# Key rows and row sums of v from TensorE with 0/1 matrices, in place of a DRAM staging copy

## The chip, the cores and the metric

The kernel runs on one core of a Trainium2 chip. The metric is the device time of one execution in microseconds, taken as the median of several runs. The profile is one further execution with the hardware profiler on.

## The reference

Three stages, each of which feeds the next. Only the first one is touched here.

```python
# q, k, v: (4, 8, 576, 64): batch, heads, sequence, head width
q_d, k_d, v_d = (t.reshape(B, H, 144, 4, 64).mean(axis=3) for t in (q, k, v))
out_d  = softmax(q_d @ k_d.T / 8) @ v_d          # each row repeated 4 times
local  = where(abs(i - j) < 4, q @ k.T / 8, -1e9)
x      = repeat(out_d, 4) + softmax(local) @ v   # -> (2304, 512) tokens
g = x @ w_gate; x = (silu(g) * (x @ w_val)) @ w_out          # 512 -> 1536 -> 512
h = x @ w_in;   out = (max(h,0) + alpha*min(h,0)) @ w2_out   # 512 -> 2048 -> 512
```

So for v the first stage needs two things: the sums of four neighbouring rows (for the coarse attention), and, for each query, the seven key rows around it (for the local attention).

## The kernel before

**Attention.** Work comes in units: unit n is one pair of heads and half a sequence (288 rows). There are 4 units per half sequence and 32 in all. The first sequence is units 0 to 7: units 0 to 3 are the first half of its four head pairs, 4 to 7 the second half. They are called the prologue here and are written out by `a_all`: transposes of k and q on TensorE (`a_T`, L283 and L286, L292 for units 4 to 7), scores (`a_QK`, L334 local and L338 coarse, then L343 to L360), exponentials (`a_EXP`, L368 and L377), row sums and normalisation with the 32x32 transposes into the block diagonal tile bd (`a_NRM`, L386 to L408), the transpose of the coarse weights (`a_PT`, L415, L418), and the products with v (`a_PV`, L435 coarse, L439 local, L443 to L449), whose result goes as a high and a low part (xh, xl) to the next stage.

**The two forms of v.** The local product L439 takes vw: for each block of 24 queries the 32 rows of v around it, four blocks in the 128 partitions. `stage(b)` writes these windows for the whole sequence b into a DRAM tensor, vwin (L246 to L261), and `a_load_w` reads them back, two DMAs a unit (L237). The coarse product L435 takes vs, sums of four rows of v: `a_load_v` loads v again as 72 rows of four (tile vd, L216), and `a_vd` adds them on GpSimd (L321, L322), for units 0 to 3; units 4 to 7 use the same sums.

**The order at the start.** SyncE's queue is in order and carries every DMA: k and q of units 0 to 3 (L202, L207), stage(0), the four vd, the windows (L237) and the weights of the first four of twelve column groups j (L103, L105; three tiles g, v, o of 512 KB for each j). Each weight tile is split on arrival into a high and a low part (`w_split`): ScalarE L126, VectorE L127 and L128, ScalarE L131, GpSimd L132. The main loop takes, for each block of 288 tokens and each j, 12 matmuls for gate (L462 to L464), 12 for value and 12 for the output product, with VectorE L502 and L508 between them. A scheduler with a model of the chip's times fixes the order of instructions on each engine beforehand, within the dependences and a few gates; on the chip each engine keeps that order.

**Buffers.** PSUM holds four tiles of two banks for the prologue, one for each of units 0 to 3; units 4 to 7 share three of them, so that unit 7 comes after unit 4. In SBUF the prologue lives in weight slots that are not loaded yet: `order` is g4 v4 o4 g5 (q and vw), v5 o5 g6 v6 (qs: transposed q, scores, results), o6 g7 v7 o7 (k, later q and vw of units 4 to 7), g8 v8 o8 g9 (vd, later qs of units 4 to 7), v9 o9 g10 v10 (bd). A weight tile is loaded once its slot is given back.

Of the kernel before, what the change touches and what calls it, by code (L numbers as in the profile page):

```python
# [8 lines left out]
F32 = mybir.dt.float32  # L9
# [3 lines left out]
ALU = mybir.AluOpType  # L13
# [4 lines left out]

K = dict(kdP=0, qdP=0, dnP=2, ldn=9, lo='asvw0123', NPRO=8, c=5, a1=1, a2=0, OFF=25, oT=3, oE=3, oP=5, oV=11, vd1=2, vd2=1, pre=(1, 1, 0, 0), lo1=0, lo2=1, nst=3, nrm=0, sub=0, nrm1=0, sub1=0, qtA=0, ldw=1, xl1=0, ly=4, l2=3, st2=2, early=1, w2p=1, la=0, bdV=0, sp=9, s2=0, s3=0, gj=7, gs=1, vr=0, kc=0, gD=(0, 0, 0, 0, 0, 0), gP=(0, 2, 8, 8, 0, 0), gA=(0, 0, 0, 0, 0, 0))


@with_exitstack
def attn_moe_moe2_kernel(
# [113 lines left out]
    pbd = {}  # L137
    kds = {}
    vss = {}
    vds = {}  # L140
    bds = [ap_.tile([128, 2, NW, 128], F32, name=f"bd{i}", bufs=1) for i in range(NBD)]

    def coords(n):
        blk, hp = divmod(n, NP)
        b, half = divmod(blk, 2)
        return b, half, hp, blk
# [1 line left out]
    order = [f"{kind}{j}" for j in range(F1 - 8, F1) for kind in "gvo"]  # L148
    st_slots = order[5 * NP:][:K["nst"]]
    NEARLY = F1 - 2  # L150
    pslot = {(what, n): order[4 * i + n] for i, what in enumerate(("qv", "qs", "kn", "vd", "bd")) for n in range(NP)}
    for n in range(NP):
        pslot["qv", n + NP] = pslot["kn", n]
        pslot["qs", n + NP] = pslot["qs" if K["vr"] else "vd", n]
    NPRO = K["NPRO"]
    srs = [ap_.tile([128, 8], F32, name=f"sr{i}", bufs=1) for i in range(4)]

    def at_(n, shape, tag):
        return wp.tile(shape, F32, tag=pslot[tag, n], name=tag)
# [23 lines left out]
    def a_load(n):  # L183
        b, half, hp, blk = coords(n)
        h0, t0 = 2 * hp, half * HB
        d = hu[n] = {}
        if n >= NPRO:

            loads = [("qn", q, HB, t0)]
            if half == 0:  # L190
                loads.insert(0, ("kn", k, S, 0))
            for tag, src, rn, r0 in loads:
                t = d[tag] = ap_.tile([128, rn], F32, tag=tag, name=tag, bufs=1)
                for i in range(4):
                    nc.sync.dma_start(
                        out=t[32 * i:32 * (i + 1)].rearrange("r (m c) -> r m c", c=32),
                        in_=src[b, h0 + i // 2, r0:r0 + rn, 32 * (i % 2):32 * (i % 2 + 1)].rearrange("(m r) c -> r m c", r=32))
            return
        if half == 0:
            kn = d["kn"] = at_(n, [QB, 6, 2, D], "kn")  # L200
            for h in range(2):
                nc.sync.dma_start(out=kn[:, :, h], in_=k[b, h0 + h].rearrange("(r p) c -> p r c", p=QB))  # L202
        t = at_(n, [128, 2 * NW * 2 * D], "qv").rearrange("p (a w h c) -> p a w h c", a=2, w=NW, h=2)
        d["vw"] = t[:, 1]
        qn = d["qn"] = t[:QB, 0]
        for h in range(2):
            nc.sync.dma_start(out=qn[:, :, h], in_=q[b, h0 + h, t0:t0 + HB, :].rearrange("(r p) c -> p r c", p=QB))  # L207

    def a_load_v(n):
        b, half, hp, blk = coords(n)  # L210
        h0 = 2 * hp
        if half == 0:
            hu[n]["vd"] = []
            if n < NP:
                vd = vds[hp] = at_(n, [72, 2, 2, 4 * D], "vd")
                nc.sync.dma_start(out=vd.rearrange("p h f x -> p (h f) x"),  # L216
                                  in_=v[b, h0:h0 + 2].rearrange("h (f p r) c -> p (h f) (r c)", f=2, r=4))
            for f in range(2):
                if n < NP:
                    hu[n]["vd"].append(vd[:, :, f])  # L220
                    continue
                vf = ap_.tile([72, 2, 4 * D], F32, tag="vd", name="vd", bufs=NVD)
                hu[n]["vd"].append(vf)
                nc.sync.dma_start(out=vf, in_=v[b, h0:h0 + 2, f * HB:(f + 1) * HB].rearrange("h (p r) c -> p h (r c)", r=4))

    def a_load_w(n):

        b, half, hp, blk = coords(n)
        if n < NP:
            pbd[n] = at_(n, [128, 2, NW, 128], "bd")  # L230
            (nc.vector if K["bdV"] else nc.gpsimd).memset(pbd[n], 0.0)
        if n >= NPRO:
            hu[n]["vw"] = ap_.tile([128, NW, 2, D], F32, tag="vw", name="vw", bufs=NVW)
        t = hu[n]["vw"]
        for h in range(2):
            w0 = ((b * H + 2 * hp + h) * 2 + half) * NW * 128
            nc.sync.dma_start(out=t[:, :, h], in_=vwin[w0:w0 + NW * 128, :].rearrange("(w p) c -> p w c", p=128))  # L237

    def stage(b):

        nw = H * S // SUB
        g0, g1, ng = b * nw, (b + 1) * nw, B * nw

        def win(a, e):
            n = (e - a) * SWIN
            nc.sync.dma_start(  # L246
                out=vwin[a * SWIN:e * SWIN, :].rearrange("(g r) c -> g (r c)", r=SWIN),
                in_=bass.AP(v.tensor, v.offset + (a * SUB - 3) * D, [[SUB * D, e - a], [1, SWIN * D]]))

        vf = v.rearrange("b h s c -> (b h s) c")  # L250
        if g0 == 0:
            nc.sync.dma_start(out=vwin[0:3, :], in_=vf[0:3, :])
            nc.sync.dma_start(out=vwin[3:SWIN, :], in_=vf[0:SWIN - 3, :])
            win(1, 16)
            g0 = 16
        if g1 == ng:
            win(g0, g1 - 16)
            win(g1 - 16, g1 - 1)
            r0, m = (g1 - 1) * SWIN, SUB + 3
            nc.sync.dma_start(out=vwin[r0:r0 + m, :], in_=vf[B * H * S - m:, :])  # L260
            nc.sync.dma_start(out=vwin[r0 + m:r0 + SWIN, :], in_=vf[0:SWIN - m, :])  # L261
        else:
            win(g0, g1)
# [48 lines left out]

    def a_vd(n):
        b, half, hp, blk = coords(n)
        if n < NPRO and K["vr"]:
            return
        if half == 0:
            vs = vss[hp] = ap_.tile([72, 2, 2, D], F32, tag=f"vs{hp}", name="vs", bufs=1)
            for f in range(2):
                vv = hu[n]["vd"][f].rearrange("p h (r c) -> p h r c", r=4)  # L320
                nc.gpsimd.tensor_tensor(out=vv[:, :, 0:2], in0=vv[:, :, 0:2], in1=vv[:, :, 2:4], op=ALU.add)  # L321
                nc.gpsimd.tensor_tensor(out=vs[:, f], in0=vv[:, :, 0], in1=vv[:, :, 1], op=ALU.add)  # L322

    def a_QK(n, A):
        b, half, hp, blk = coords(n)
# [94 lines left out]
    def a_PV(n, A):  # L420
        b, half, hp, blk = coords(n)
        d = hu[n]
        pt, vw, bd = d["pt"], d["vw"], d["bd"]
        if n < NPRO and K["vr"]:
            vd = vds[hp].rearrange("p h f (r c) -> p h f r c", r=4)
            for f in range(2):
                for r in range(4):
                    for h in range(2):
                        nc.tensor.matmul(A[64 * h:64 * h + 64, 1, 0:QD], vd[:, h, f, r], pt[:, h, f * QD:(f + 1) * QD],
                                         start=(f == r == 0), stop=(f == 1 and r == 3))  # L430
        else:
            vs = vss[hp]
            for f in range(2):
                for h in range(2):
                    nc.tensor.matmul(A[64 * h:64 * h + 64, 1, 0:QD], vs[:, f, h], pt[:, h, f * QD:(f + 1) * QD],  # L435
                                     start=(f == 0), stop=(f == 1))
        for w in range(NW):
            for h in range(2):
                nc.tensor.matmul(A[64 * h:64 * h + 64, 0, w * QB:(w + 1) * QB], vw[:, w, h],  # L439
# [31 lines left out]
    def load1(j):  # L471
        for kind in "gvo":
            w_load(kind, j, f"{kind}{j}")
# [144 lines left out]

    if True:
        make_identity(nc, ident)  # L620
        for tok in K["lo"]:
            if tok == "s":
                stage(0)
            elif tok in "avw":
                for n in range(NP):
                    {"a": a_load, "v": a_load_v, "w": a_load_w}[tok](n)
            elif tok == "x":
                for n in range(NP):
                    a_load_v(n)
                    a_load_w(n)  # L630
            else:
                load1(int(tok))
        for t in srs:
            nc.vector.memset(t, 1.0)

# [17 lines left out]
        P = [ATT, Y[0], Y[1], pgv.tile([128, 2, 512], F32, name="gv")]  # L653
        def a_all(n, A):
            a_T(n, A)
            if K["vd1"] == 0:
                a_vd(n)
            a_QK(n, A)
            gate(n, 0)
            if K["vd1"] == 1:  # L660
                a_vd(n)
            a_EXP(n)
            a_NRM(n)
            gate(n, 1)
            if K["vd1"] == 2:
                a_vd(n)
            a_PT(n, A)
            if K["vd1"] == 3:
                a_vd(n)
            a_PV(n, A)  # L670

        pc = [0]
# [13 lines left out]
        GV[1] = pg2.tile([128, 512], F32, name="v")  # L686
        for n in range(NP, NPRO):
            a_load(n)
            a_load_w(n)
        for n in range(NP, NPRO):  # L690
            if n == NP + 2:
                preps(K["pre"][2])
# [141 lines left out]
```

## Time and profile before

| | |
|---|---|
| median of 3 runs | 1025.0 us (1024.01 to 1026.19) |
| the profiled execution | 1022.0 us |
| span of its profile | 1020.1 us |
| TensorE busy | 970.3 us, 95% |
| VectorE, GpSimd, ScalarE busy | 496.7, 387.7, 292.3 us |

The shares are means over the whole span. The prologue and the first block of the main loop, roughly the first 150 us, look quite different from the rest, and the rows further down are mostly from there. A matmul's duration in the trace includes its latency, so a TensorE that is "busy" is not one at its peak.

### The profile page before, as it was taken

Reading aid. Unit: us, or ns where it says so; the run is one execution under the profiler, and the core shown is the slowest. Engines: PE = TensorE matmul, PEld = TensorE weight load, DVE = VectorE, ACT = ScalarE, POOL = GpSimd, SP = SyncE. Lnnn points to the kernel's source line nnn. Section 1 sums busy time; section 2 is a strip of 40 time slices with the busy share of each in tenths; the row PEclk is TensorE's granted clock in tenths of the full one; section 3 lists DMA queues with packets and bytes.
Section 4 is the critical chain, followed back from the end, with each engine's and each line's share of the span. In section 5 each row is a group of like instructions: output and inputs, shape, how many; then the busy total and the mean of one; then the engine's idle time right before and its main releaser. Section 6 shows DMA issues by size and latency. Waiting matters only on the chain.

```text
span 1020.1 us, 19253 instructions
## 1 busy us (share of the span) xinstructions
PE 970.3 (95%) x7760; PEld 867.5 (85%) x7760; DVE 496.7 (49%) x1045; ACT 292.3 (29%) x660; POOL 387.7 (38%) x492
## 2 busy tenths in 40 slices
PE   5388789999999999999999999999999999999997
PEld 4288789999999999999999998888888888888896
DVE  5898884546453646353532769722322322322232
ACT  3656542222222222222223656312101101111111
POOL 5868773233422343322223335724223322322222
PEclk9999999999999999999999999999999999999999
DMA  8996751123120232110103884102000100100010
GB/s 199 289 305 217 196 139 39 35 67 60 42 51 16 54 71 45 38 29 15 43 13 88 290 265 127 42 1 62 21 0 19 55 1 1 42 11 0 1 43 21
DMA packets 135895, 77.81 MB, mean 76 GB/s; under 512 B 97407, under 2 KB 127103, under 8 KB 135039
## 3 DMA queue, kind: packets, MB, share of 16 engines
q1 hardware_dynamic: 135804, 76.58, 27.0%
q8 instruction: 60, 0.98, 0.4%
q14 instruction: 31, 0.25, 0.1%
HBM read 67.12 MB, written 15.73 MB: 81 GB/s over the span
## 4 chain that ended last, share of the span: by engine, by line
PE 79%; DVE 7%; DMA 6%; SPq 4%; issue 2%; POOL 2%; ACT 1%; DVEq 0%; POOLq 0%; ACTq 0%
PE y L599 6%; PE y L601 6%; PE y L600 6%; PE g L462 6%; PE v L463 6%; PE v L462 5%; PE g L464 5%; PE g L463 5%; PE v L464 5%; PE y L462 4%; PE y L464 4%; PE y L463 4%; PE h L462 3%; PE h L464 3%; PE h L463 3%
## 5 line engine op out<-in xcount | busy, mean ns | idle before, releaser
L587 POOL TENSOR_TENSOR gl<-t,gh 128x512 fp32r<-128x512 f32 (+1 forms) x80 | 97.0, 1214 | 250.6 <-ACT gh L586 244.1
L462 PE MATMUL g<-xh,w 128*128 128x288 f32 x384 | 117.0, 305 | 13.4 <-DVE u L502 8.8
L586 ACT CAST gh<-t 128x512 fp32r<-128x512 f32 (+1 forms) x80 | 46.1, 578 | 278.4 <-DVE t L583 239.0
L463 PE MATMUL y<-pl,w 128*128 128x288 f32 x384 | 114.3, 300 | 3.2 <-POOL pl L512 3.2
L462 PE MATMUL v<-xh,w 128*128 128x288 f32 x384 | 116.5, 303 | 0.0
L463 PE MATMUL v<-xl,w 128*128 128x288 f32 x384 | 116.0, 302 | 0.0
L464 PE MATMUL g<-xh,w 128*128 128x288 f32 x384 | 114.6, 298 | 1.2 <-POOL w L132 1.2
L464 PE MATMUL v<-xh,w 128*128 128x288 f32 x384 | 114.7, 299 | 0.0
L463 PE MATMUL g<-xl,w 128*128 128x288 f32 x384 | 114.6, 298 | 0.0
L599 PE MATMUL y<-w,gh 128*128 128x512 f32 x288 | 113.2, 393 | 1.0 <-ACT sy L531 1.0
L502 DVE SCALAR_TENSOR_TENSOR u<-u,g 128x288 f32<-128x288 f32 x96 | 43.3, 451 | 144.2 <-ACT u L501 144.1
L464 PE MATMUL y<-ph,w 128*128 128x288 f32 x384 | 113.5, 298 | 0.0
L600 PE MATMUL y<-w,gh 128*128 128x512 f32 x288 | 112.8, 392 | 0.0
L601 PE MATMUL y<-w,gl 128*128 128x512 f32 x288 | 112.0, 392 | 0.0
L462 PE MATMUL y<-ph,w 128*128 128x288 f32 x384 | 111.2, 303 | 0.3 <-ACT ph L511 0.3
L512 POOL TENSOR_TENSOR pl<-u,ph 128x288 fp32r<-128x288 f32 x96 | 80.8, 842 | 56.0 <-ACT ph L511 55.7
L132 POOL TENSOR_TENSOR w<-st,w 128x512 fp32r<-128x512 f32 x52 | 73.8, 1425 | 59.5 <-ACT w L131 57.8
L462 PEld LDWEIGHTS g<-xh,w 128*128 128x128 f32 x384 | 73.2, 191 | 16.8 <-DVE u L502 10.8
L581 DVE TENSOR_SCALAR t<-h,alpha 128x512 f32<-128x512 f32 (+1 forms) x40 | 27.9, 697 | 110.7 <-PE h L464 109.5
L463 PEld LDWEIGHTS y<-pl,w 128*128 128x128 f32 x384 | 72.4, 189 | 4.4 <-POOL pl L512 3.9
L462 PEld LDWEIGHTS y<-ph,w 128*128 128x128 f32 x384 | 71.0, 189 | 5.1 <-issue 4.2
L463 PEld LDWEIGHTS v<-xl,w 128*128 128x128 f32 x384 | 73.5, 191 | 1.7
(188 smaller groups left out, 2116.3 us busy)
## 6 DMA issues: line engine op xcount, KB each, us to landing
raw<-in_moe_w_out_dram SPq DMA_DIRECT2D x28, 512.0 KB, 4.5
raw<-in_moe_w_in_dram SPq DMA_DIRECT2D x16, 512.0 KB, 5.2
raw<-in_moe_w_gate_dram SPq DMA_DIRECT2D x12, 512.0 KB, 9.5
raw<-in_moe_w_val_dram SPq DMA_DIRECT2D x12, 512.0 KB, 8.7
vw<-vwin SPq DMA_DIRECT2D x48, 96.0 KB, 2.4
out_dram<-os SPq DMA_DIRECT2D x18, 256.0 KB, 2.5
sy<-y SPq DMA_DIRECT2D x16, 256.0 KB, 2.9
y<-ys SPq DMA_DIRECT2D x14, 288.0 KB, 2.9
```

What stands on the lines that cost most here:

```text
L132: eng.tensor_sub(w[:, 1], st, f32(w[:, 0]))
L462: nc.tensor.matmul(o, lhi, rhi, start=first, stop=False)
L463: nc.tensor.matmul(o, lhi, rlo, start=False, stop=False)
L464: nc.tensor.matmul(o, llo, rhi, start=False, stop=last)
L502: nc.vector.scalar_tensor_tensor(out=u, in0=u, scalar=1.0, in1=GV[0][:, :HB], op0=ALU.add, op1=ALU.mult)
L512: nc.gpsimd.tensor_sub(pl, u, f32(ph))
L581: nc.vector.tensor_scalar(out=t[:, :n], in0=P[:, :n], scalar1=0.0, scalar2=alpha_sb[:, j:j + 1], op0=ALU.min, op1=ALU.mult)
L586: nc.scalar.copy(out=gh[:, :n], in_=t[:, :n])
L587: nc.gpsimd.tensor_sub(gl[:, :n], t[:, :n], f32(gh[:, :n]))
L599: nc.tensor.matmul(o, gh[:, ms], ohi, start=(j == 0), stop=False)
L600: nc.tensor.matmul(o, gh[:, ms], olo, start=False, stop=False)
L601: nc.tensor.matmul(o, gl[:, ms], ohi, start=False, stop=(j == F2 - 1))
```

## The change

For units 0 to 7 v is loaded once for each head pair, as a tile vn of 104 partitions: rows 96r - 3 to 96r + 100 for each of six blocks r of 96 rows, both heads. Two 0/1 matrices are built on GpSimd: selw copies the right 104 rows into the 128 window rows, sel4 adds rows by fours. A new step `a_V`, between `a_EXP` and `a_NRM`, multiplies with them on TensorE, into the unit's own PSUM tile, and ScalarE copies the results to vw and vs. stage(0), the vd tiles, the window loads and the GpSimd sums of units 0 to 7 go. The vn tile takes the slots of vd (g8 v8 o8 g9), and units 4 to 7 now use the qs slots of units 0 to 3 (v5 o5 g6 v6). Later sequences are as before.

```diff
     for n in range(NP):
         pslot["qv", n + NP] = pslot["kn", n]
-        pslot["qs", n + NP] = pslot["qs" if K["vr"] else "vd", n]
+        pslot["qs", n + NP] = pslot["qs", n]
...
+        vn = vns[hp] = at_(n, [VR, S // QB, 2, D], "vn")
+        for h in range(2):
+            r0 = (b * H + h0 + h) * S - 3
+            a = max(0, -r0)
+            nc.sync.dma_start(out=vn[a:, :, h],
+                              in_=bass.AP(v.tensor, v.offset + (r0 + a) * D, [[D, VR - a], [QB * D, S // QB], [1, D]]))
...
-        if g0 == 0:
-            nc.sync.dma_start(out=vwin[0:3, :], in_=vf[0:3, :])
-            nc.sync.dma_start(out=vwin[3:SWIN, :], in_=vf[0:SWIN - 3, :])
-            win(1, 16)
-            g0 = 16
...
+    def a_V(n, A):
+
+        b, half, hp, blk = coords(n)
+        vn = vns[hp].rearrange("p r h c -> p r (h c)")
+        nc.tensor.matmul(A[:, 0, 0:NW * 128], selw, vns[hp].rearrange("p r h c -> p (r h c)")[:, half * NW * 128:(half + 1) * NW * 128],
+                         start=True, stop=True)
+        nc.scalar.copy(out=hu[n]["vw"].rearrange("p w h c -> p (w h c)"), in_=A[:, 0, 0:NW * 128])
+        if half == 0:
+            for f in range(2):
+                for r in range(NW):
+                    nc.tensor.matmul(A[:72, 1, f * 128:(f + 1) * 128], sel4[:, r], vn[:, NW * f + r],
+                                     start=(r == 0), stop=(r == NW - 1))
+            vs = vss[hp] = ap_.tile([72, 2, 2, D], F32, tag=f"vs{hp}", name="vs", bufs=1)
+            nc.scalar.copy(out=vs.rearrange("p f h c -> p (f h c)"), in_=A[:72, 1, 0:256])
...
-        for tok in K["lo"]:
-            if tok == "s":
-                stage(0)
-            elif tok in "avw":
-                for n in range(NP):
-                    {"a": a_load, "v": a_load_v, "w": a_load_w}[tok](n)
...
+        for n in range(NP):
+            a_load(n)
+        for j in range(4):
+            load1(j)
+        for n in range(NP):
+            pbd[n] = at_(n, [128, 2, NW, 128], "bd")
+            nc.gpsimd.memset(pbd[n], 0.0)
+
+        nc.gpsimd.memset(selw, 0.0)
+        nc.gpsimd.affine_select(out=selw.rearrange("p (i r) -> p i r", i=NS), in_=selw.rearrange("p (i r) -> p i r", i=NS),
+                                pattern=[[-SUB, NS], [-1, SWIN]], compare_op=ALU.not_equal, fill=1.0, base=0, channel_multiplier=1)
+        nc.gpsimd.memset(sel4, 1.0)
+        nc.gpsimd.affine_select(out=sel4, in_=sel4, pattern=[[QB, NW], [-4, 72]], compare_op=ALU.is_ge, fill=0.0,
+                                base=-3, channel_multiplier=1)
...
             a_QK(n, A)
             gate(n, 0)
-            if K["vd1"] == 1:
-                a_vd(n)
             a_EXP(n)
+            a_V(n, A)
             a_NRM(n)
             gate(n, 1)
-            if K["vd1"] == 2:
-                a_vd(n)
             a_PT(n, A)
             a_PV(n, A)
...
         for n in range(NP, NPRO):
             a_load(n)
-            a_load_w(n)
```

sel4 takes four such selects in all. `a_load` returns for units 4 to 7 before the load of vn.

## Rows read from the trace of the kernel before

**Rows 1.** The page: busy time and share of each engine.

```profile
PE 970.3 (95%) x7760; PEld 867.5 (85%) x7760; DVE 496.7 (49%) x1045; ACT 292.3 (29%) x660; POOL 387.7 (38%) x492
```

**Rows 2.** By stretch: length, busy PE, PEld, DVE, ACT, POOL, PEclk, DMA share, GB/s.

```profile
5.00:10.00 5.00, 3.47 (x65) 2.55 (x63) 1.73 (x4) 1.92 (x2) 3.54 (x22) 1.00 1.05 207
10.00:20.00 10.00, 8.81 (x183) 6.71 (x181) 9.59 (x32) 4.93 (x16) 1.53 (x3) 1.00 0.79 219
20.00:30.00 10.00, 2.67 (x22) 1.61 (x22) 2.08 (x7) 2.45 (x9) 8.55 (x16) 1.00 1.08 282
30.00:52.00 22.00, 7.98 (x78) 6.03 (x76) 21.41 (x41) 15.07 (x37) 17.75 (x22) 1.00 0.93 268
60.00:140.00 80.00, 68.89 (x783) 62.71 (x783) 72.19 (x146) 45.60 (x111) 58.31 (x63) 0.94 0.74 231
140.00:160.00 20.00, 19.82 (x205) 18.86 (x203) 12.04 (x30) 7.79 (x18) 13.01 (x19) 1.00 0.45 107
```

**Rows 3.** Timeline of VectorE, then of ScalarE, around the first weight tile.

```profile
10.26 0.36 DVE L343 TENSOR_TENSOR qs<-att,mask 128x192 f32<-128x192 f32 x1 [0.94 <-PE att L338]
...
29.23 1.06 DVE L127 TENSOR_SCALAR st<-st 128x512 int32<-128x512 int32 x1 [7.92 <-ACT st L126]
...
28.53 0.67 ACT L126 ACTIVATE st<-raw 128x512 f32<-128x512 f32 x1 [6.66 <-DMA raw<-in_moe_w_gate_dram]
```

**Rows 4.** DMA issues of the first 60 us, with KB of each.

```profile
vwin<-in_v_dram SPq DMA_DIRECT2D x2, 1408.0 KB
...
qv<-vwin SPq DMA_DIRECT2D x16, 96.0 KB, 4.9
...
kn<-in_k_dram SPq DMA_DIRECT2D x8, 144.0 KB
qv<-in_q_dram SPq DMA_DIRECT2D x16, 72.0 KB, 2.9
vd<-in_v_dram SPq DMA_DIRECT2D x4, 288.0 KB
```

**Rows 5.** SyncE's queue, timeline.

```profile
84.36 20.47 SPq L103 DMA_DIRECT2D raw<-in_moe_w_out_dram  x2
...
113.89 0.39 SPq L105 DMA_DIRECT2D raw<-in_moe_w_gate_dram  x1
```

**Rows 6.** GpSimd: two groups of the first 60 us, then its timeline.

```profile
L321 POOL TENSOR_TENSOR vd<-vd 72x256 f32<-72x256 f32 x8 | 5.6, 720 | 3.6 <-DMA vd<-in_v_dram 3.6
L322 POOL TENSOR_TENSOR vs<-vd 72x128 f32<-72x128 f32 x8 | 4.1, 530 | 0.0
...
3.00 0.29 POOL masks.py:199 TENSOR_SCALAR_AFFINE_SELECT ident<-ident 128x128 f32<-128x128 f32 x1
...
7.54 1.31 POOL L648 COPY mask<-tmp 32x128 f32<-32x128 f32 x4
```

**Rows 7.** Timeline of TensorE.

```profile
10.60 1.16 PE L283 MATMUL y<-ident,kn 96*128 96x96 f32 x6
...
46.89 1.23 PE L439 MATMUL gv<-bd,qv 128*64 128x96 f32 x12
51.73 0.61 PE L462 MATMUL g<-xh,w 128*128 128x288 f32 x1 [3.62 <-DVE qs L444]
...
103.78 0.67 PE L439 MATMUL att<-bd,qv 128*64 128x96 f32 x12
```

**Rows 8.** VectorE by source line from 20 us on: ns min/median/max, first and last start.

```profile
L127 DVE TENSOR_SCALAR st<-st x36: 372/598/2512, 29.2 to 142.3; 128x512 int32<-128x512 int32 x36
...
L128 DVE SCALAR_TENSOR_TENSOR st<-raw,st x36: 649/742/1719, 30.5 to 143.8; 128x512 int32<-128x512 int32 x36
```

**Rows 9.** Timeline of ScalarE: a copy from PSUM, and two late weight tiles.

```profile
11.76 0.64 ACT L289 COPY kT<-y 128x576 f32<-128x576 f32 x1 [3.22 <-DVE qs L288]
...
117.60 1.25 ACT L126 ACTIVATE st<-raw 128x512 f32<-128x512 f32 x2 [1.87 <-POOL w L132]
```

**Rows 10.** Waits of TensorE, 58 to 145 us: total, times, longest.

```profile
PE g L462 <- DVE u L502: 7.3, 6, 2.1
```

More of the change, by code (lines that the diff above doesn't have):

```diff
@@ L139, in attn_moe_moe2_kernel @@
     vss = {}
-    vds = {}
+    vns = {}
+    VR = QB + 8
     bds = [ap_.tile([128, 2, NW, 128], F32, name=f"bd{i}", bufs=1) for i in range(NBD)]
@@ L150, in attn_moe_moe2_kernel @@
     NEARLY = F1 - 2
-    pslot = {(what, n): order[4 * i + n] for i, what in enumerate(("qv", "qs", "kn", "vd", "bd")) for n in range(NP)}
+    pslot = {(what, n): order[4 * i + n] for i, what in enumerate(("qv", "qs", "kn", "vn", "bd")) for n in range(NP)}
     for n in range(NP):
         pslot["qv", n + NP] = pslot["kn", n]
-        pslot["qs", n + NP] = pslot["qs" if K["vr"] else "vd", n]
+        pslot["qs", n + NP] = pslot["qs", n]
     NPRO = K["NPRO"]
+    selw = ap_.tile([VR, 128], F32, name="selw", bufs=1)
+    sel4 = ap_.tile([VR, NW, 72], F32, name="sel4", bufs=1)
     srs = [ap_.tile([128, 8], F32, name=f"sr{i}", bufs=1) for i in range(4)]
@@ L207, in a_load @@
             nc.sync.dma_start(out=qn[:, :, h], in_=q[b, h0 + h, t0:t0 + HB, :].rearrange("(r p) c -> p r c", p=QB))
+        if half:
+            return
+        vn = vns[hp] = at_(n, [VR, S // QB, 2, D], "vn")
[4 more added lines that the diff above has]
+                              in_=bass.AP(v.tensor, v.offset + (r0 + a) * D, [[D, VR - a], [QB * D, S // QB], [1, D]]))
+            if a:
+                nc.gpsimd.memset(vn[:a, 0, h], 0.0)
+                nc.sync.dma_start(out=vn[:a, 1:, h],
+                                  in_=bass.AP(v.tensor, v.offset + (r0 + QB) * D, [[D, a], [QB * D, S // QB - 1], [1, D]]))
     def a_load_v(n):
@@ L213, in a_load_v @@
             hu[n]["vd"] = []
[L214 to L217, printed above, removed]
             for f in range(2):
-                if n < NP:
-                    hu[n]["vd"].append(vd[:, :, f])
-                    continue
                 vf = ap_.tile([72, 2, 4 * D], F32, tag="vd", name="vd", bufs=NVD)
@@ L228, in a_load_w @@
         b, half, hp, blk = coords(n)
[L229 to L234, printed above, removed]
+        t = hu[n]["vw"] = ap_.tile([128, NW, 2, D], F32, tag="vw", name="vw", bufs=NVW)
         for h in range(2):
@@ L314, in a_vd @@
         b, half, hp, blk = coords(n)
-        if n < NPRO and K["vr"]:
-            return
         if half == 0:
@@ L423, in a_PV @@
         pt, vw, bd = d["pt"], d["vw"], d["bd"]
[L424 to L436, printed above, removed]
+        vs = vss[hp]
+        for f in range(2):
+            for h in range(2):
+                nc.tensor.matmul(A[64 * h:64 * h + 64, 1, 0:QD], vs[:, f, h], pt[:, h, f * QD:(f + 1) * QD],
+                                 start=(f == 0), stop=(f == 1))
         for w in range(NW):
@@ L620, in attn_moe_moe2_kernel @@
         make_identity(nc, ident)
-        for tok in K["lo"]:
-            if tok == "s":
-                stage(0)
-            elif tok in "avw":
-                for n in range(NP):
-                    {"a": a_load, "v": a_load_v, "w": a_load_w}[tok](n)
-            elif tok == "x":
-                for n in range(NP):
-                    a_load_v(n)
-                    a_load_w(n)
-            else:
-                load1(int(tok))
+        for n in range(NP):
[11 more added lines that the diff above has]
+                                base=-3, channel_multiplier=1)
+        nc.gpsimd.affine_select(out=sel4, in_=sel4, pattern=[[-QB, NW], [4, 72]], compare_op=ALU.is_ge, fill=0.0,
+                                base=6, channel_multiplier=-1)
+        nc.gpsimd.affine_select(out=sel4, in_=sel4, pattern=[[-24, NW], [1, 72]], compare_op=ALU.is_ge, fill=0.0,
+                                base=0, channel_multiplier=0)
+        nc.gpsimd.affine_select(out=sel4, in_=sel4, pattern=[[24, NW], [-1, 72]], compare_op=ALU.is_ge, fill=0.0,
+                                base=23, channel_multiplier=0)
         for t in srs:
@@ L655, in a_all @@
             a_T(n, A)
-            if K["vd1"] == 0:
-                a_vd(n)
             a_QK(n, A)
             gate(n, 0)
-            if K["vd1"] == 1:
-                a_vd(n)
             a_EXP(n)
+            a_V(n, A)
             a_NRM(n)
             gate(n, 1)
-            if K["vd1"] == 2:
-                a_vd(n)
             a_PT(n, A)
-            if K["vd1"] == 3:
-                a_vd(n)
             a_PV(n, A)
@@ L688, in attn_moe_moe2_kernel @@
             a_load(n)
-            a_load_w(n)
         for n in range(NP, NPRO):
```

## The prediction

> **What bounds the kernel now.** I read the page first: TensorE is busy for 95% of the span [rows 1]. So a change in the first 160 us is worth what it moves the moment from which TensorE never stops again, and nothing else. The second view, the busy time by stretch, finds that moment: from 140 us on TensorE works 19.82 of 20 us, while from 60 to 140 us it works 68.89 of 80, and from 10 to 52 us it is idle for 1.19 + 7.33 + 14.02 = 22.5 us [rows 2]. In the stretch from 30 to 140 us VectorE is the full engine: 21.41 of 22 us, then 72.19 of 80. TensorE's longest waits there are for VectorE's L502, 7.3 us in six waits [rows 10]: the gate's function is queued behind the splitting of weights. The last of the 36 weight tiles reaches VectorE at 142.3 us [rows 8], which is where TensorE becomes full. So the early phase ends when VectorE has got through the splits and the attention steps of the prologue.
>
> The third view is VectorE's timeline. Before the first split it pauses for 7.92 us, from 21.3 to 29.2 us, while ScalarE waits for the first gate tile from DMA [rows 3]. In the stretch from 20 to 30 us VectorE works 2.08 us, and the DMA engines are full (share 1.08) [rows 2]. What they carry then is the subject of the change.
>
> **The change, step by step.** *DMA ahead of the first weight tile.* Before, the queue carries k (8 x 144 = 1152 KB), q of units 0 to 3 (8 x 72 = 576), stage(0) (1408 and three small ones that I leave out), vd (4 x 288 = 1152), one window load (96) and the tile itself (512): 4896 KB [rows 4], landed at 28.5 us, so 172 KB/us. After, stage(0), vd and window loads go, and vn comes: 104 rows x 6 blocks x 256 bytes = 156 KB a head, 1248 KB in eight loads (a ninth is three rows). Ahead of and with the first tile there are then 1152 + 576 + 1248 + 512 = 3488 KB, and at the same 172 KB/us it lands at 20.3 us, 8.2 us earlier. From both sides: at the 207 GB/s that the small rows of k and q reach from 5 to 10 us and 282 GB/s for the weight tile [rows 2] it would be 14.7 + 1.9 = 16.6 us; if vn runs at half of 207 it is 8.5 + 12.3 + 1.9 = 22.7 us. Each lies ahead of 28.5.
>
> *VectorE's pause.* With the tile at 20.3 us and 0.67 us on ScalarE, L127 can begin at 21.0, before the pause now opens at 21.3. The pause of 7.9 us is worth **-7.9 us**; with the tile at 22.7, 5.6. VectorE's own work is unchanged: the change adds and removes nothing on it.
>
> *GpSimd, removed.* The sums L321 and L322 of four head pairs, 5.6 + 4.1 = 9.7 us [rows 6], go. Most of it lies inside VectorE's pause. Behind them in the same queue stand L360 and L397 of units 1 to 3, which then run as soon as VectorE asks; that is the work which fills the time ahead of 21 us. VectorE also gets freer of GpSimd: L127 on one and the same shape takes 372 ns at best, 598 in the middle, 2512 at worst [rows 8]. I take **-0.5 us**, between 0 and -1.8 (9.7 less the 7.9 of the pause). [...]
>
> *GpSimd, added.* Two memsets and five selects for the 0/1 matrices stand ahead of the mask in the program. The nearest row is the select of ident, 128 elements, 0.29 us [rows 6]; seven of these with up to 216 elements are 2.0 to 3.4 us, I take 2.4. The mask, complete at 7.54 + 1.31 = 8.85, is then there at 11.25, and the first use, L343, began at 10.26 [rows 3]: **+1.0 us**, from 0 (if the scheduler puts the mask first) to 3.4. Behind L343 queue the other VectorE steps of unit 0.
>
> *TensorE, added.* An f32 product stands in the trace as two records (L439: 12 for six products). Six records of 96 columns take 1.16 us in L283, 2.0 ns a column at full width; L439 gives 1.07 ns a column, but with 64 of the 128 weight columns [rows 7]. By the first, key rows cost 384 x 2 x 2.0 = 1.5 us a unit and the sums 6 x 128 x 2 x 2.0 = 3.1 us a head pair. In units 0 to 3 that is 4 x 4.6 = 18.4 us, in idle time of 22.5 us (above): covered, but narrowly. If that cover were gone, unit 3 would end that much later; weight splits would still fill VectorE. In units 4 to 7 it is 4 x 1.5 = 6.0 us, or half of it at the later pace (the 12 records of L439 take 0.67 us at 104 us against 1.23 at 47), beside 11.1 us of idle TensorE from 60 to 140 us: **+1.0 us**, between 0 and 3.0.
>
> *ScalarE, added.* A copy of 128x576 from PSUM takes 0.64 us [rows 9]. By elements the eight of 384 cost 0.43 each and the four of 256 0.28: 4.6 us, on an engine that is busy for 15.07 of 22 and 45.60 of 80 us. Nothing, at most +0.5: the copy stands ahead of the coarse normalisation in the same queue, but VectorE and GpSimd work on the local one meanwhile.
>
> *SyncE.* Some 24 issues go, 9 come; k and q of units 2 and 3 are issued behind the vn of units 0 and 1. VectorE has unit 0 and 1 to work on by then, so I add nothing beyond the terms above. The four products that L435 and L439 make are as before.
>
> Sum: -7.9 - 0.5 + 1.0 + 1.0 = **-6.4 us**. Against the profiled execution, 1022.0 us (span 1020.1 and 1.9 around it), that is 1015.6. The median of the runs is 3.0 us above that execution, so I forecast 1018.6 us as a median. Its own range by the bounds is -9.7 to about 0 us, 1015 to 1025.
>
> **The rivals.** *The slots are given back too late.* Units 4 to 7 now hold the slots v5, o5, g6, v6 until their end; before, they held g8, v8, o8, g9. Unit 7 is late: its product with v ran at 103.8 us [rows 7], SyncE's queue stood 20.47 us behind the output tile that waits for it, and the next gate tile, behind unit 7's last step, was issued at 113.9 [rows 5] and taken by ScalarE at 117.6 [rows 9]. That tile belongs to j = 9. Under the change v6, the 20th tile of 36, has this place. If unit 7 ends as late as now and VectorE's queue keeps the tiles' order, 16 tiles come after 117.6. At the median pair, 0.60 + 0.74 us, they end at 139; at the present rate of one in 3.2 us (113.1 us for 35) at 169. A third of the way up, at 149, the early phase ends 7 us late, and with the +2.0 of the added work less the 0.5 the median is 1033.5; with unit 7 some 6 us earlier, for its earlier q, 1027.5. I price it between them, at 1030. For it: unit 7's lateness comes from a full VectorE, which stays full. Against: q of units 4 to 7 no longer waits behind window loads, so unit 7 begins earlier. The point from which it decides: with 2.3 us a tile, between the two paces, 16 tiles take 37 us, so v6 must be at ScalarE by 105 us to end at 142.3, and unit 7 must end 3.7 us (117.6 less 113.9) before that, at 101; six us earlier than that it takes nothing of the forecast.
>
> *The pause only moves.* Orders are fixed ahead. If the first split is placed ahead of steps of units 2 and 3, or if these units now wait for TensorE (18.4 us into 22.5), VectorE stands still somewhere else for about as long. Then -7.9 falls away in most part and the median stays near 1025, between 1023 and 1027. For it: that is how the pause arises now, with one late tile at the queue's head. Against: the tile's new time lies ahead of the pause.
>
> *The later waits shrink too.* The block of products that begins at 51.73 us [rows 7] waits for attention results of units 0 to 3, which had waited for the windows. If it begins over ten us earlier, gate and value run ahead of the splits, and part of the 11.1 us of idle TensorE goes as well: 6 us more, 1012.6. Against: VectorE, not TensorE, is full there.
>
> **How the numbers follow.** Forecast 0.50, moved pause 0.19, late slots 0.16, later waits 0.15. About 0.2%, 2 us, is what a measurement can tell here. Faster: 0.48 of the forecast, all 0.15, 0.03 of the moved pause, 0.66; same: 0.02 + 0.13, 0.15; slower: 0.16 + 0.03, 0.19. The range reaches from 1011, under the case with fewer waits, to 1030, at the price of the late slots; about half of the latter lies above it.
>
> **What would show it.** Right: the first gate tile on ScalarE at 17 to 23 us; no pause of VectorE over 3 us between 15 and 30; the last L127 near 136; L462 beginning before 49. Wrong: a pause of VectorE elsewhere, a long wait of SyncE's queue ahead of v6 with TensorE waiting for a split of j = 6, or a first L343 later than 13 us. What would make the prediction wrong above all is a new order on the engines that I can't see from here.

## The result

| | before | changed kernel |
|---|---|---|
| median | 1024.51 us | 1034.49 us (1033.66 to 1034.97) |
| profiled execution, span | 1022.0, 1020.1 us | 1034.37, 1032.6 us |
| ratio to before | | 1.0097, 95% interval 1.0077 to 1.0117 |

The change makes the kernel about 1% slower. The forecast was 1018.6 us, between 1011 and 1030: the sign is wrong and the time lies outside.

The time is lost in the first 20 us and again after 100 us. SyncE's queue shows the first (start and length of each issue, us):

```profile
2.84 0.36 SPq L218 DMA_DIRECT2D vn<-in_v_dram  x1
3.25 8.38 SPq L222 DMA_DIRECT2D vn<-in_v_dram  x1
11.67 0.31 SPq L218 DMA_DIRECT2D vn<-in_v_dram  x1
12.02 1.02 SPq L205 DMA_DIRECT2D kn<-in_k_dram  x2
...
23.43 1.75 SPq L105 DMA_DIRECT2D raw<-in_moe_w_gate_dram  x1
```

L218 is the first of v's loads, 101 partitions (the first head has no rows ahead of it). The load behind it, three partitions of L222, stands 8.38 us without waiting for any semaphore; k of unit 1, issued at 2.78 us before, follows at 12.02. The busy time by stretch, first of the changed kernel, then one line of before, shows what the DMA engines did in between (last columns: granted TensorE clock, DMA share, GB/s):

```profile
6.00:8.00 2.00, 0.00 (x0) 0.00 (x0) 0.89 (x3) 1.47 (x2) 2.00 (x9) 1.00 0.08 18
8.00:10.00 2.00, 1.40 (x52) 0.96 (x52) 0.75 (x1) 0.45 (x1) 1.85 (x7) 1.00 0.08 18
10.00:12.00 2.00, 0.05 (x2) 0.00 (x0) 0.00 (x0) 0.00 (x0) 0.71 (x3) 1.00 0.08 18
```

```profile
6.00:8.00 2.00, 1.19 (x6) 0.93 (x6) 0.97 (x3) 1.38 (x2) 1.81 (x7) 1.00 1.03 201
```

A share of 0.08 is about one engine of 16 (1/16 is 0.06). The 151.5 KB of the 101-partition load take some 8.6 us at 18 GB/s; the load behind it has under 4 KB and can't be what runs that long. What waits for it (timelines of TensorE, VectorE and ScalarE of the changed kernel):

```profile
16.46 1.22 PE L282 MATMUL y<-ident,kn 96*128 96x96 f32 x6 [6.41 <-DMA kn<-in_k_dram]
```

```profile
18.19 0.36 DVE L286 COPY qs<-y 128x192 f32<-128x192 f32 x1 [8.96 <-PE y L285]
```

```profile
29.37 0.67 ACT L126 ACTIVATE st<-raw 128x512 f32<-128x512 f32 x1 [1.71 <-DMA raw<-in_moe_w_gate_dram]
```

The pause of VectorE [rows 3] has not gone: it is 8.96 us, ten us earlier, and the first gate tile reaches ScalarE at 29.37 (before 28.53). The stretches that answer to [rows 2] say the rest:

```profile
10.00:20.00 10.00, 1.75 (x11) 1.41 (x9) 1.77 (x6) 0.64 (x1) 0.71 (x3) 1.00 0.84 148
20.00:30.00 10.00, 9.15 (x101) 7.12 (x101) 7.09 (x24) 4.63 (x16) 2.03 (x4) 1.00 1.09 227
30.00:52.00 22.00, 18.75 (x188) 13.05 (x188) 20.50 (x46) 18.66 (x50) 14.24 (x13) 1.00 1.02 310
60.00:140.00 80.00, 68.81 (x642) 60.31 (x643) 68.19 (x140) 45.95 (x114) 54.51 (x65) 0.86 0.68 201
```

From 10 to 20 us TensorE works 1.75 us (before 8.81) and VectorE 1.77 (before 9.59). From there attention of units 0 to 3 runs among the weight splits; the first gate product, at 51.73 us before [rows 7], starts at 66.91:

```profile
66.91 0.59 PE L466 MATMUL g<-xh,w 128*128 128x288 f32 x1
```

The last split starts at 146.6 us (143.8 before [rows 8]). The last copy of block 0's results starts at 164.71 us; before, the last two copies stand in one row that starts at 150.22 (timelines of ScalarE, the changed kernel, then before):

```profile
164.71 0.63 ACT L535 COPY ys<-y 128x576 f32<-128x576 f32 x1
```

```profile
150.22 1.36 ACT L531 COPY ys<-y 128x576 f32<-128x576 f32 x2
```

From the last copy to the end little changes: 1032.6 - 164.71 = 867.9 us, and 1020.1 - (150.22 + 0.68) = 869.2 before. The loss stands ahead of it.

### The profile page after: what moved, and what is told of

Read it like the earlier page. It is cut to its first block, busy times and chain, and to the rows that moved or that the text cites. A ratio compares the mean times of both kernels' runs of the same rounds, so it can differ in the third digit from the quotient of the medians.

```text
span 1032.6 us, 19355 instructions
## 1 busy us (share of the span) xinstructions
PE 988.7 (96%) x7824; PEld 877.9 (85%) x7824; DVE 492.1 (48%) x1045; ACT 295.1 (29%) x672; POOL 375.6 (36%) x484
## 4 chain that ended last, share of the span: by engine, by line
PE 79%; DVE 7%; DMA 4%; POOL 3%; issue 2%; ACT 2%; SPq 2%; DVEq 0%; POOLq 0%; ACTq 0%
PE y L603 6%; PE y L605 6%; PE y L604 6%; PE g L466 6%; PE v L467 6%; PE v L466 5%; PE g L468 5%; PE g L467 5%; PE v L468 5%; PE y L466 4%; PE y L468 4%; PE y L467 4%; PE h L466 3%; PE h L468 3%; PE h L467 3%
## 5 line engine op out<-in xcount | busy, mean ns | idle before, releaser
L132 POOL TENSOR_TENSOR w<-st,w 128x512 fp32r<-128x512 f32 x52 | 71.2, 1373 | 68.5 <-ACT w L131 67.0
L466 PEld LDWEIGHTS v<-xh,w 128*128 128x128 f32 x384 | 73.3, 191 | 3.5 <-DVE u L512 1.7
```

The source lines that it names most:

```text
L132: eng.tensor_sub(w[:, 1], st, f32(w[:, 0]))
L466: nc.tensor.matmul(o, lhi, rhi, start=first, stop=False)
```

## The experiments

Eleven kernels ran, in four sets, each set beside runs of before on its own chip. Ratios carry the comparison. "Split load" means that v's first load, of 101 partitions, is made as 104, 96 and 5 partitions; "early slots" is explained at its run. All times but the medians are from the profiles: first gate tile on ScalarE, first gate product on TensorE, start of the last split on VectorE, start of the last copy of block 0, and TensorE's busy time from 100 to 120 us.

| kernel | median | ratio to before, 95% interval | gate tile | gate product | last split | last copy | PE 100-120 |
|---|---|---|---|---|---|---|---|
| before | | | 28.5 | 51.7 | 143.8 | 150.9 | 17.30 |
| changed | 1034.5 | 1.0097 (1.0077-1.0117) | 29.4 | 66.9 | 146.6 | 164.7 | 14.94 |
| e1 split load | 1026.8 | 1.0037 (1.0024-1.0051) | 22.4 | 59.4 | 139.7 | 157.7 | 13.20 |
| e2 before + lone load | 1039.4 | 1.0154 (1.0137-1.0171) | 36.5 | 57.9 | 159.2 | 170.7 | 17.53 |
| e3 e1, k and q first | 1027.3 | 1.0038 (1.0023-1.0053) | 21.1 | 58.4 | 141.6 | 159.5 | 13.44 |
| e4 e1, no sums | 1022.6 | 1.0000 (0.9985-1.0015) | 22.4 | 57.4 | 137.7 | 152.5 | 13.29 |
| e5 e1, early slots | 1021.0 | 0.9978 (0.9967-0.9988) | 21.7 | 59.5 | 132.5 | 152.8 | 17.31 |
| e7 e1, sums twice | 1028.6 | 1.0055 (1.0042-1.0069) | 22.5 | 56.9 | 147.1 | 159.3 | 12.54 |
| e9 e1, splits held back | 1037.7 | 1.0149 (1.0132-1.0166) | 22.6 | 49.7 | 148.7 | 170.6 | 12.46 |
| e10 e5, no sums | 1024.8 | 1.0017 (1.0006-1.0027) | 22.8 | 57.9 | 138.0 | 156.4 | 16.95 |
| e11 changed, early slots | 1030.2 | 1.0069 (1.0052-1.0086) | 29.5 | 67.2 | 139.6 | 158.2 | 19.06 |
| e12 e5, k and q first | 1019.2 | 0.9963 (0.9949-0.9977) | 21.4 | 58.5 | 138.8 | 151.5 | 18.90 |
| e13 e5, sums twice | 1022.6 | 0.9986 (0.9972-1.0000) | 21.8 | 56.7 | 136.8 | 152.6 | 17.54 |

(Where the trace joins both copies into one row, half its length is added to its start.)

### Is it the load of 101 partitions?

Theory A: the load runs on one DMA engine and holds up the queue. Rival B: TensorE's added products and the new order cost the time, whatever the load does. First set, e1 to e4.

```diff
-nc.sync.dma_start(out=vn[a:, :, h], in_=...)          # 101 partitions, 6 blocks
-nc.sync.dma_start(out=vn[:a, 1:, h], in_=...)         # 3 partitions, 5 blocks
+nc.sync.dma_start(out=vn[:, 1:, h], in_=...)          # 104 partitions, 5 blocks
+nc.sync.dma_start(out=vn[8:, 0, h], in_=...)          # 96 partitions
+nc.sync.dma_start(out=vn[a:8, 0, h], in_=...)         # 5 partitions
```

> The changed kernel with the first load of vn cut differently: blocks 1 to 5 from all 104 partitions, block 0 as 96 and 5 partitions, in place of one load of 101 partitions and one of 3. Theory A (the 101-partition load ran on one DMA engine at 18 GB/s, the next issue of SyncE's queue stood 8.38 us behind it, and all later loads moved back by that): k of unit 1 is issued near 4.5 us in place of 12.0, the first gate tile reaches ScalarE near 22 in place of 29.4, and the time falls by 7 to 9 us, to about 1026. Theory B (the products with the 0/1 matrices fill TensorE in the prologue and set the end of unit 3): the loads move as said, but the first L466 moves by under 4 us and the time stays above 1030. My forecast of before would ask for 1018.6.

```profile
2.84 0.47 SPq L220 DMA_DIRECT2D vn<-in_v_dram  x1
3.36 0.41 SPq L222 DMA_DIRECT2D vn<-in_v_dram  x1
3.81 0.32 SPq L224 DMA_DIRECT2D vn<-in_v_dram  x1
4.18 0.33 SPq L227 DMA_DIRECT2D vn<-in_v_dram  x1
4.55 1.01 SPq L205 DMA_DIRECT2D kn<-in_k_dram  x2
```

```profile
6.00:8.00 2.00, 0.05 (x1) 0.00 (x0) 0.97 (x3) 1.30 (x2) 2.00 (x9) 1.00 1.30 207
```

```profile
22.38 0.66 ACT L126 ACTIVATE st<-raw 128x512 f32<-128x512 f32 x1 [1.59 <-DMA raw<-in_moe_w_gate_dram]
```

The same queue without the stall, the DMA engines full, the gate tile 7.0 us earlier. By the ratios the load's form is worth 0.60%, 6.1 us, a little under the 7 to 9 expected. B's sign, a first gate product moved by under 4 us, did not come: it moved by 7.5. A holds; but the kernel still stands 0.37% above before, so there is a second cause. What no run separates is whether the stall comes from the number 101 or from something else in the form of this load, such as its start at partition 3.

```diff
 # kernel before, ahead of k of unit 1: two loads that nobody uses
+xn = wp.tile([104, 6, 2, D], F32, tag="o11", name="xn")
+nc.sync.dma_start(out=xn[3:, :, 0], in_=...)          # 101 partitions, 6 blocks
+nc.sync.dma_start(out=xn[:3, 1:, 0], in_=...)         # 3 partitions, 5 blocks
```

> The kernel before with two more loads behind q of unit 0, of 101 and of 3 partitions, into a free slot that nothing reads; all results are as before. Theory A: SyncE's queue stands about 8.4 us at the second of them, and the time rises by 7 to 9 us, to about 1033. Rival (the prologue of the kernel before has slack for a late queue, and the loss of the change has another cause): the queue stands as long, the time rises by under 3 us.

```profile
3.19 8.17 SPq L212 DMA_DIRECT2D xn<-in_v_dram  x1
```

```profile
8.00:10.00 2.00, 0.74 (x48) 0.64 (x48) 0.75 (x1) 0.41 (x1) 0.71 (x3) 1.00 0.08 18
```

The stall and the 18 GB/s came into the kernel of before with the load alone, and the gate tile moved by 8.0 us, as A says. The end moved by 1.54%, 15.8 us, twice what was expected. Its last split is 15.4 us late; why the stall doubles on its way through the splits stays open.

```diff
 # e1, with the loads in another order
+for n in range(NP): a_load(n)       # k and q of units 0 to 3
+for n in range(NP): a_load_n(n)     # then v's tiles
```

> e1 with k and q of all four units ahead of all vn loads. If units 2 and 3 wait for their k and q behind vn (theory A's rest), it is 1 to 3 us faster than e1. If TensorE sets the end of unit 3 (theory B), or if the key rows of unit 0 are wanted earlier than k of unit 3, it is the same as e1 or up to 3 us slower.

No difference to e1: where k and q of units 1 to 3 stand in the queue is not the second cause.

```diff
 # e1, the six products of the sums left out; vs is filled from key rows
-for f in range(2):
-    for r in range(NW):
-        nc.tensor.matmul(A[:72, 1, f * 128:(f + 1) * 128], sel4[:, r], vn[:, NW * f + r], ...)
-nc.scalar.copy(out=vs..., in_=A[:72, 1, 0:256])
+nc.scalar.copy(out=vs..., in_=A[:72, 0, 0:256])
```

> e1 without the products with sel4: vs is filled from the key rows, so the coarse attention multiplies with wrong values and the output is not the reference's. Theory B (TensorE's added products in the prologue are the price): without 4 x 2.8 us of them units 1 to 3 end earlier, the first L466 by 5 us or more, and the time falls by 4 us or more against e1. Theory A alone: within 2 us of e1.

3.8 us less than e1 by the ratios, but the first gate product comes only 2.0 us earlier, where B asked for 5 or more. The time alone made it look as if B were half right. The second set questions that.

### What is the second cause?

The rows from 100 to 120 us pointed to the slots: TensorE works 13.20 of 20 us in e1 and 13.29 in e4, against 17.30 before. GpSimd's last step of unit 7 and SyncE's queue in the changed kernel show why:

```profile
109.53 0.98 POOL L453 TENSOR_TENSOR xl<-qs,xh 128x288 fp32r<-128x288 f32 x1
```

```profile
110.54 0.39 SPq L105 DMA_DIRECT2D raw<-in_moe_w_val_dram  x1
```

A tile of the value weights is issued 0.03 us after unit 7 ends (109.53 + 0.98 = 110.51). In the kernel before the tile at this place is one of the gate weights [rows 5], g9; here it must be v6, whose slot unit 7 holds. In e1 the pair stands at 103.65 and 103.67. e5 changes which slots are held:

```diff
-("qv", "qs", "kn", "vn", "bd")
+("qv", "vn", "kn", "qs", "bd")     # in pslot: v's tile takes v5, o5, g6, v6; q, exp and x take g8, v8, o8, g9
```

v's tile is given back by the key-row product of units 4 to 7, early in each unit.

> The split load, and two groups of slots change places: the four slots of q, exp and x (held to unit 7's end) become those of weight tiles 8 and 9, and v's tile (given back by the key-row product of units 4 to 7) takes those of tiles 5 and 6. Theory of the late slots: in the split-load run TensorE was busy only 13.20 us of 100 to 120 (before 17.30), because v5, o5, g6 and v6 come late; TensorE's share of that stretch comes back to about 17 us and the time falls by 2 to 4 us, to about 1023 to 1025. Rival, the pause only moves and TensorE's own added work pays: loads come earlier, time stays within 1 us of the split-load run (1026.8).

```profile
100.00:120.00 20.00, 17.31 (x147) 16.09 (x145) 15.66 (x26) 11.56 (x24) 15.76 (x13) 1.00 0.86 236
```

```profile
L128 DVE SCALAR_TENSOR_TENSOR st<-raw,st x36: 649/693/1821, 22.8 to 132.5; 128x512 int32<-128x512 int32 x36
```

TensorE has its 17.31 us back, the last split comes 7.2 us earlier than in e1, and the time falls by 0.59%, 6.0 us: more than the 2 to 4 expected. Unit 7 itself ends no earlier than in e1, at 104.94 + 0.99 = 105.93 us; what changed is which tile waits for it, again one of the gate weights:

```profile
104.94 0.99 POOL L458 TENSOR_TENSOR xl<-qs,xh 128x288 fp32r<-128x288 f32 x1
```

```profile
106.65 0.40 SPq L105 DMA_DIRECT2D raw<-in_moe_w_gate_dram  x1
```

So the slots were the second cause. The version is 0.22% below before, 2.3 us. Only the medians show that gain. The two profiled executions have the same span, 1020.1 us: block 0's last copy comes 1.9 us later than before (152.8 for 150.9), and what follows it is 1.9 us shorter.

```diff
 # e1, with the products of the sums made twice
-for r in range(NW):
+for r in 2 * list(range(NW)):
```

> The split load, with the row sums' products of units 0 to 3 made twice over (the second set overwrites the first with the same result): 24 more products, 6.6 us of TensorE by the rows of the split-load run (1.5 to 1.8 us for 12 records of one unit). If the sums' products stand on the path, as the run without them said (4.1 us less), this costs again about 4 us: 1030 to 1032. If that run gained for another reason (the granted clock stayed at its upper level from 30 to 60 us), twice the products cost less than 2 us: 1027 to 1029.

0.18% over e1, 1.8 us: the products double, and the cost is under half of what e4 gave back. It falls on the side of "less than 2 us".

```diff
-gD=(0, 0, 0, 0, 0, 0)
+gD=(0, 8, 8, 8, 0, 0)     # splits of tiles 1 to 3 behind unit 3's normalisation on VectorE
```

> The split load, and the splits of weight tiles 1 to 3 may start only after VectorE's last normalizing instruction of unit 3. Theory, that the earlier splits push the attention of units 2 and 3 back (first gate product at 59.44 us, before 51.73): the first gate product comes back to about 53 us, and the time falls by 3 us or more if that start sets the end of block 0. Rival, that VectorE's total sets it: the pause comes back as idle time of VectorE before 40 us, and the time is the same or rises, by up to 6 us.

```profile
49.66 0.61 PE L471 MATMUL g<-xh,w 128*128 128x288 f32 x1
```

```profile
30.00:40.00 10.00, 10.00 (x62) 7.04 (x63) 5.84 (x20) 7.79 (x25) 5.12 (x8) 1.00 1.09 308
```

The first gate product is 9.8 us earlier than in e1 and 2.1 earlier than before, and the kernel is 11.5 us slower than e1. VectorE works 5.84 of the 10 us from 30 to 40 (9.81 in e1), and the last split has gone from 139.7 to 148.7. The rival holds in kind, though it allowed for 6 us at most: here an early start of TensorE is worth nothing, and the splits end later.

### Do the causes add, and what do the sums cost?

```diff
 # e4, with
-("qv", "qs", "kn", "vn", "bd")
+("qv", "vn", "kn", "qs", "bd")
```

> The split load and the changed places of the slots, without the row sums' products (the buffer of sums is filled from key rows instead, so the output is not the reference's). If the three causes add (the load on one DMA engine, the slots held long, the products of the sums), the products' 4.1 us come off this version too: 1016.5 to 1018.5, beside 1021.0 with them. Rival: what the sums cost was TensorE's lower clock or its start at a point where it waited for late weights, and with the weights early that is covered: 1020 to 1021.5.

e4 with the places of e5. It is 4.0 us slower than e5 by the ratios, and neither theory expected that. TensorE waits for VectorE's gate function (waits of e10 from 60 to 160 us, then of e5; total, times, longest):

```profile
PE g L467 <- DVE u L507: 9.2, 5, 4.2
```

```profile
PE g L471 <- DVE u L511: 3.6, 3, 1.5
```

At the longest of these waits, up to 135.07 us, the gate function (134.58) stands on VectorE behind two steps of splits (131.12 and 133.27) and steps of later units. I read the 4.0 us as the effect of a new order, which the missing work brings with it; no run shows that apart. So e4's 3.8 us can't be read as the price of the products.

```diff
 # the changed kernel, with
-("qv", "qs", "kn", "vn", "bd")
+("qv", "vn", "kn", "qs", "bd")
```

> The changed kernel as it is, its 101-partition load kept, with only the slots' places changed. If the two causes add, the slots are worth 5 to 6 us here as in the split-load version: 1028 to 1030 (the changed kernel 1034.5). Rival: with the splits 8 us later, weights that come earlier are not wanted earlier, and the time stays above 1032.

The changed kernel with only the slots moved: 1030.2 us, 0.28% or 2.9 us less, with TensorE back at 19.06 us from 100 to 120. The gain is only just clear of the noise (the intervals of e11 and of the changed kernel overlap, 1.0052 to 1.0086 and 1.0077 to 1.0117). The two causes don't simply add: the slots are worth 2.9 us with the stall and 6.0 without, and the load's form 6.1 us with the late slots and 9.3 with the early ones (from 1.0069 to 0.9978).

```diff
 # e5, with
+for n in range(NP): a_load_n(n)     # v's tiles behind k and q of units 0 to 3
```

> The split load and the changed places of the slots, with k and q of all four units issued ahead of v's tiles. The work is the same as in the version with early slots (1021.0); only the order of the loads differs, and with it the order of the instructions that is laid out. If that order alone moves the time by several us, this run differs from 1021.0 by 2 us or more, either way; if not, 1020 to 1022.

e5 with e3's order of loads. The fastest version: 0.37% below before, at 1019.2 us, and 1.5 us below e5 by the ratios (the intervals overlap). The order alone moved less than 2 us.

```profile
100.00:120.00 20.00, 18.90 (x169) 18.02 (x165) 15.57 (x26) 11.84 (x25) 15.88 (x13) 1.00 0.83 234
```

```diff
 # e5, with
-for r in range(NW):
+for r in 2 * list(range(NW)):
```

> The split load, the changed places of the slots, and the row sums' products twice over. If these products carry a price of their own of 2 us or more (the split-load version with them twice was 1.9 us slower), 1023 or more, as there. Rival, that the runs without them and with them twice differ by the order of the instructions around them and not by their time: the sign can be any, and 1019 to 1022 speaks for it.

0.8 us over e5 by the ratios, with intervals that overlap; the median, 1022.6, falls between the two forecasts. Twice the sums cost 1.8 us in one setting and 0.8, perhaps nothing, in the other; leaving them out gave 3.8 us in one and took 4.0 in the other. So the products cost little, under 2 us for a second set. That the 3.8 and the 4.0 us are the work of a new order is argued, not shown.

## Why the prediction was wrong, step by step

- **SyncE, "I add nothing beyond the terms above": the step that failed first.** I counted nine loads, "a ninth is three rows", and took all of v's bytes at the pace of loads that keep the engines full (207 GB/s at a share of 1.05 [rows 2]): the slow bound was half of 207 GB/s. The load of 101 partitions ran at 18. The gate tile, forecast for 20.3 us, came at 29.4; with the load split it came at 22.4, inside the bounds 16.6 to 22.7. With it fell the sum's term of -7.9: VectorE's pause stayed, at 8.96 us, and the mask was first used at 19.12 us, past the 13 that the prediction gave as a sign of being wrong. The load's form costs 6.1 to 9.3 us. That it ran on one engine is my reading of the DMA share: 0.08 from 6 to 12 us in the changed kernel and in e2, against 1.30 from 6 to 8 us in e1, whose loads have 104, 96 and 5 partitions. Why it ran so was not shown.
- **The late slots: a rival at 16% that happened as well.** Its deciding point was v6 at ScalarE by 105 us, unit 7 ended by 101. Unit 7 ended at 103.65 in e1 and 110.51 in the changed kernel, both too late. Its price, 11.4 us over the forecast, was too high: 6.0 us without the stall, 2.9 with it. Together with the stall it passes the range's top of 1030.
- **VectorE's pause, -7.9.** Its first half was right: with the load split no pause over 2.5 us is left between VectorE's first instruction and the splits, and the gate tile lies in its bound. The second half, that the whole pause comes off the end, was not. The last split comes 4.1 us earlier than before in e1 (139.7 for 143.8); with early slots it is 11.3 us in e5, but 5.0 in e12. And in e5 the time comes off only in part: block 0 takes 93.3 us from its first gate product to its last copy (99.2 before), but begins 7.7 us later.
- **What bounds the phase: "the early phase ends when VectorE has got through the splits" was too simple.** e9 speaks for it: gate products earlier, splits later, and 11.5 us lost. But in e1 the last split starts 4.1 us earlier than before and block 0's last copy 6.8 us later, and e12's last split is 6.3 us later than e5's, its last copy 1.3 us earlier. So an earlier end of the splits does not by itself bring an earlier end of block 0. The later start of the gate products goes with splits that now stand among the attention steps: held back in e9, they let it begin at 49.7 us. What else sets the end of block 0 stays open.
- **TensorE's added products, "covered, but narrowly".** The sums of units 0 to 3 take 10.0 us in e5 (2.77, 2.83, 2.84 and 1.53), forecast 12.4; key rows take 1.65 us for a unit at their longest, forecast 1.5. From 10 to 52 us TensorE is idle for 7.2 us in e5, and e9, with all these products, has its first gate product 2.1 us earlier than before. The cover held.
- **GpSimd, added +1.0.** The mask is complete at 10.14 + 0.62 = 10.76 us, forecast 11.25, and VectorE's first use of it is in e1 at 12.82 us, behind other work: nothing. The -0.5 for the sums that GpSimd no longer makes was not tried apart, and neither was a version with these sums back on GpSimd, so that half of the change has no run of its own.
- **Pause only moves; later waits shrink too.** The first is what the trace of the changed kernel shows, but by the load and not by a late product or order as I had argued. The second asked for gate products over ten us earlier; in all versions but e9 they were later than before.

The design that I forecast, without the two defects, is e5: 2.3 us below before by its ratio, where the sum said 6.4. e12, with the loads in another order too, is 3.8 us below. Its median of 1019.2 us lies 0.6 us from the forecast, but that is luck: the kernel before was faster beside it, 1023.4 us for the 1025.0 that the forecast started from, and the sum's terms did not come out as priced. Between the sum (-6.4 us) and the result (+10.0) lie 16.4 us; the load's form and the slots together account for 12.2 of them (from 1.0097 to 0.9978), and the other 4.1 stay open.

## What to carry to other kernels

When a change alters the shape of a load, look at the pace of each load before the sum of the bytes: one load of 101 partitions at the head of a queue, at 18 GB/s, brought the first weight tile 7.0 us later (29.4 for 22.4), more than the lighter queue saved (28.5 to 22.4). When slots are handed on, write down which load waits for the last user of each; a swap of two names in a list was worth 6.0 us in one setting and 2.9 in another. And where the order is laid out by a planner, taking work out is no clean measure of its price: try it both ways and in two settings.

## What the runs showed of the hardware that was not expected

- The queue of SyncE stood 8.38 us (8.17 in e2) at the issue behind the 101-partition load, with no semaphore to wait for, while the DMA share was 0.08 (6 to 12 us in both); the next issue came at 11.67 us (11.40 in e2). So in these two runs the queue was late as a whole, and not only those who wanted the slow transfer's data.
- TensorE's granted clock was 1.00 from 30 to 52 us in the kernel before and in the changed one, but 0.64 in e1 (0.66 from 30 to 40 us, 0.64 from 40 to 50 and 0.50 from 50 to 60). In the 10 us ahead of that TensorE was busy for 2.67 us before, 9.15 in the changed kernel and 10.00 in e1. But e12 was busy for 10.00 us there too, and its clock stayed at 1.00 from 30 to 60 us, so what made it fall in e1 stays open. In e4 and e10 the clock was 1.00 throughout 30 to 60 us, and one was faster and the other slower than its partner with the sums, so the clock alone did not decide either.
- Gate and value products follow each other at 0.24 us in e1 from 59.8 to 63.2 us, where the granted clock is 0.50 (50 to 60 us) and 0.83 (60 to 70 us), and at 0.13 us from 78 to 79.3 us, where it is 1.00 (70 to 80 us). But in the kernel before they follow at 0.24 us from 52.1 to 57.4 us as well, and there the granted clock is 1.00 (52 to 58 us). The granted clock alone does not give their pace.
